# Whole turns of a phase by one write to int32 in place of two float steps, in a gated attention with two gated MLPs

## The chip, the core and the metric

The kernel runs on one core of a Trainium2 chip. Five engines work side by side, each in the order of its own queue: TensorE (PE, with its weight loads as PEld), VectorE (DVE), ScalarE (ACT), GpSimd (POOL) and SyncE (SP, which here only issues DMA transfers). The metric is the device time of one execution in microseconds, lower is better. Times are medians of several runs.

## The reference

The input is q, k, v and complex gates a for 4 x 8 heads, 768 positions and 48 channels. Then come two gated MLPs over 3072 tokens (384 to 2048 to 384).

```python
mag = sqrt(a_re**2 + a_im**2)
scale = minimum(mag, 0.999) / (mag + 1e-6)
a = (a_re + 1j * a_im) * scale                 # per head, position and channel
for t in range(768):
    S = a[:, :, t, :, None] * S + k[t] (outer) v[t]
    y[t] = q[t] @ S.real
x = y as 3072 x 384
x = (h * clip(h + 3, 0, 6) / 6) @ w_out,   h = x @ w_in          # first MLP
x = (h * sigmoid(1.702 * h)) @ w_out,      h = x @ w_in          # second MLP
```

The recurrence is computed in chunks of 128 positions: within a chunk the products of the gates are a decay (the running sum of log magnitudes) and a phase (the running sum of angles). q and k are multiplied by exp(+-decay) and by the cosine and the sine of the phase, and after that the chunk is plain matrix products with a causal mask.

## The kernel before, in words

Twelve batches of 256 positions are prepared (`prep_ops`), each of two chunks; the first batch is prepared in two halves of one chunk each (tokens that end in `.0.0` and `.0.1`), so its tiles are 128 x 384 in place of 128 x 768. The steps of one batch, in the kernel's names: `im2`, `re2` (squares of the gates, ACT), `mag2`, `ln`, `mag`, `inv`, `half`, `eps`, `lneps`, `decay`, `lnhalf`, `invhalf`, `tan`, `scan` (running decay), `E0`, `E1` (its exponentials), `atan`, `carry` (adds the phase left by the batch before), `angle` (running phase), then `round`, `turns`, `frac` (takes whole turns away, so that the sine sees at most half a turn), `keep` (the phase for the next batch), `sin`, `abs`, `cos` on ACT, `qkcos` and `qksin` (q and k times cosine and sine, into the tiles pE and qk).

In `round` (L463) the half angle is scaled to turns and 12582912 is added, which leaves the whole number in the low bits; `turns` (L464) subtracts it again; `frac` (L465) subtracts the whole turns from the scaled angle.

`repE` and `repS` (`repack`, L476 to L486) then copy pE and qk by DMA, SBUF to SBUF, into the tile QK of a chunk, q and k of one head at a time: pE into partitions 0 to 47, qk into 48 to 95. Six transfers make each half. Those of the first batch are spread over three queues: SP, POOL and ACT (tokens `reqE`, `reqS` are ACT's part). With QK there, a chunk runs `kt` (turn k, PE), `sc` (scores, PE), `p` (mask, DVE), `ks` (ACT), `ud`, `pv` (PE), `um`, `ua` (state, DVE), `ysb`, `xp` or `xf`, `xh`, `xl` (its output as high and low part).

An MLP slot is `in` (18 or 9 matmuls, L634), `g1` to `g4` (gate, ACT and DVE) and `out` (L672). Weights come as float32 (`W`, L360, 768 KB each), are taken apart by `da`, `db`, `dc` on DVE (L123, L125, L127), rounded by `hi` on ACT (L380) and left over by `lo` on DVE (L389). `warm_up` (`wm`, L745) is 16 matmuls without use that start when the first cosine is there.

What sets the order: the string PLAN holds one token per step, and DVE, ACT and PE issue in exactly its order, up to the 82nd slot. SP and POOL have no order written out. There a scheduler places the transfers when the program is built, from where it expects the other engines to be. SP issues one transfer after another and stops at the first that has to wait. Transfers issued by SP and by ACT carry one of eight completion semaphores, DMAHW0 to DMAHW7, taken in turn; a transfer that gets one again waits until the transfer that had it before has landed. The tile `a` (gates of a batch, 768 KB, L399) has one buffer, so a batch's load waits for the last reader of the one before.

Of the kernel before, what the change touches and what calls it, by code (L numbers as in the profile page):

```python
# [257 lines left out]
def chunked_path(ctx: ExitStack, tc, flag, a_t, qk_t, v_t, w1i, w1o, w2i, w2o, out):  # L258

    nc = tc.nc  # L260
    V, A, G, T = nc.vector, nc.scalar, nc.gpsimd, nc.tensor
# [591 lines left out]
```

## Time and profile before

| what | before |
|---|---|
| median of 3 runs | 997.92 us (996.52 to 1000.21) |
| profiled execution, its own time | 998.55 us |
| its span, first to last instruction | 996.8 us |
| PE busy | 948.4 us (95%), 5378 matmuls |
| DVE busy | 643.9 us (65%), 919 instructions |
| ACT busy | 517.7 us (52%) |
| POOL busy | 105.8 us (11%) |
| chain that ended last | PE 89%, DVE 5%, ACT 2%, DMA 2% of the span |

How to read it: PE is the long engine, so what matters is where PE is not busy, or busy at a lower granted clock. The page's slices show that at the start alone: the first slice has PE at 1 tenth, the next two at 7 and 5, then 9 to the end; the granted clock is 9, 6, 8 and 9 tenths in the first four slices and 9 after that. DVE is the other way round: 9 tenths and more in slices 3 to 7, 2 to 5 tenths in the last ten. A group's line is line of the kernel, engine, operation, what it writes and reads, and its mean duration.

### The profile page before, as it was taken

The numbers are of one execution on the slowest core, as the hardware profiler recorded it, in microseconds if no ns is written. First come the engines' busy times: TensorE is split into PE (matmuls) and PEld (weight loads), VectorE is DVE, ScalarE is ACT, GpSimd is POOL, SyncE is SP. The second block draws the span as 40 slices with busy tenths as digits, with TensorE's granted clock in tenths as the row PEclk, the third lists the DMA queues.
The fourth block names the chain that finished last, engine by engine and source line by source line (L and its number), as shares of the span: only waits on it lengthen the run. The fifth ranks groups of instructions, "written<-read, shape, count | busy, mean of one in ns | idle before, by whom it ended". The sixth has DMA issues, their size and how long they took to land.

```text
span 996.8 us, 14418 instructions
## 1 busy us (share of the span) xinstructions
PE 948.4 (95%) x5378; PEld 804.8 (81%) x5378; DVE 643.9 (65%) x919; ACT 517.7 (52%) x860; POOL 105.8 (11%) x218
## 2 busy tenths in 40 slices
PE   1759999999999999999999999999999999999996
PEld 1648988998888888888888888888888888888885
DVE  6599999887777766877369984344454544533332
ACT  6376578777677575775325564243343432422332
POOL 1111202213312123031200000000000000000000
PEclk9689999999999999999999999999999999999999
DMA  7956214444443245232337441033353443300001
GB/s 270 283 163 196 66 49 125 131 128 128 122 118 96 72 120 128 80 97 73 72 132 240 159 151 40 1 125 128 127 190 127 158 159 127 111 1 1 32 1 35
DMA packets 70684, 113.63 MB, mean 114 GB/s; under 512 B 9936, under 2 KB 55632, under 8 KB 70608
## 3 DMA queue, kind: packets, MB, share of 16 engines
q1 hardware_dynamic: 63056, 101.02, 32.4%
q0 software_dynamic: 7168, 11.36, 4.3%
q8 instruction: 44, 0.72, 0.3%
q10 hardware_dynamic: 384, 0.26, 0.1%
q14 instruction: 32, 0.26, 0.1%
HBM read 80.22 MB, written 9.44 MB: 90 GB/s over the span
## 4 chain that ended last, share of the span: by engine, by line
PE 89%; DVE 5%; ACT 2%; DMA 2%; issue 1%; SPq 0%; POOL 0%; ACTq 0%; DVEq 0%
PE h L634 38%; PE o L672 38%; PE sc L517 4%; PE ud L563 3%; PE yps L537 3%; PE yps L539 2%; PE kt L526 1%; DMA wr<-in_w1i 1%; DMA QK<-qk 1%; DVE qk L474 1%; DVE pE L473 1%; DMA xf<-ysb 0%; DVE wi L389 0%; DVE pA L436 0%; DVE wx L127 0%
## 5 line engine op out<-in xcount | busy, mean ns | idle before, releaser
L634 PE MATMUL h<-xh,wi 128*128 128x512 f32 (+1 forms) x1248 | 364.9, 376 | 10.8 <-ACT wi L380 6.4
L672 PE MATMUL o<-gh,wo 128*128 128x512 f32 (+1 forms) x1248 | 364.2, 376 | 0.1
L634 PEld LDWEIGHTS h<-xh,wi 128*128 128x128 f32 x1248 | 228.0, 190 | 52.9 <-ACT wi L380 6.6
L672 PEld LDWEIGHTS o<-gh,wo 128*128 128x128 f32 x1248 | 227.2, 189 | 41.7 <-issue 0.9
L634 PE MATMUL h<-xl,wi 128*128 128x512 f32 (+1 forms) x624 | 233.9, 375 | 0.5 <-DVE xl L606 0.4
L672 PE MATMUL o<-gl,wo 128*128 128x512 f32 (+1 forms) x624 | 233.1, 374 | 0.0
L659 DVE TENSOR_TENSOR gl<-tt,gh 128x512 fp32r<-128x512 f32 x192 | 132.2, 690 | 84.0 <-ACT gh L654 83.7
L654 ACT ACTIVATE gh<-tt 128x512 fp32r<-128x512 f32 x192 | 121.0, 632 | 109.3 <-DVE tt L649 65.2
L649 DVE TENSOR_TENSOR tt<-tt,h 128x512 f32<-128x512 f32 x96 | 66.0, 688 | 144.8 <-ACT tt L641 144.8
L641 ACT ACTIVATE tt<-h 128x512 f32<-128x512 f32 x96 | 57.4, 598 | 172.2 <-PE h L634 167.2
L634 PEld LDWEIGHTS h<-xl,wi 128*128 128x128 f32 x624 | 118.3, 190 | 22.2 <-DVE xl L606 1.2
L672 PEld LDWEIGHTS o<-gl,wo 128*128 128x128 f32 x624 | 117.8, 189 | 21.0
L639 ACT ACTIVATE tt<-h,b 128x512 f32<-128x512 f32 x96 | 65.7, 685 | 75.5 <-PE h L634 72.1
L647 DVE SCALAR_TENSOR_TENSOR tt<-tt,h 128x512 f32<-128x512 f32 x96 | 65.2, 683 | 42.4 <-ACT tt L639 42.2
L551 POOL DMA_DIRECT2D xf<-ysb x60 | 30.9, 521 | 242.0 <-ACT ysb L543 232.1
L517 PE MATMUL sc<-QK 96*128 96x128 f32 x384 | 55.0, 291 | 0.0
L517 PEld LDWEIGHTS sc<-QK 96*128 96x128 f32 x384 | 50.8, 203 | 2.2 <-issue 0.7
L486 POOL DMA_DIRECT2D QK<-pE x70 | 35.7, 515 | 157.8 <-DVE pE L473 95.9
L521 DVE TENSOR_TENSOR p<-sc,causal 128x512 f32<-128x512 f32 x48 | 33.0, 688 | 20.7 <-PE sc L517 19.7
L537 PE MATMUL yps<-p,v 128*48 128x128 f32 (+1 forms) x384 | 40.4, 291 | 0.1
L486 POOL DMA_DIRECT2D QK<-qk x70 | 36.4, 526 | 15.6 <-issue 5.8
L603 ACT ACTIVATE xh<-xf 128x384 fp32r<-128x384 f32 x44 | 22.8, 518 | 27.8 <-DMA xf<-ysb 11.5
(111 smaller groups left out, 877.9 us busy)
## 6 DMA issues: line engine op xcount, KB each, us to landing
ws<-in_w2i SPq DMA_DIRECT2D x16, 768.0 KB, 4.4
ws<-in_w2o SPq DMA_DIRECT2D x16, 768.0 KB, 4.5
qk<-in_qk_t SPq DMA_DIRECT2D x48, 192.0 KB, 3.6
a<-in_a_t SPq DMA_DIRECT2D x11, 768.0 KB, 4.6
wr<-in_w1i SPq DMA_DIRECT2D x8, 768.0 KB, 8.3
wr<-in_w1o SPq DMA_DIRECT2D x8, 768.0 KB, 7.8
ws<-in_w1i SPq DMA_DIRECT2D x8, 768.0 KB, 4.4
ws<-in_w1o SPq DMA_DIRECT2D x8, 768.0 KB, 4.6
```

Of the source, the lines that this page charges most:

```text
L486: e.dma_start(out=dst, in_=src)
L517: T.matmul(out=sc[:, i, :], lhsT=kv_(4 * g + i), rhs=qv(4 * g + i), start=True, stop=True)
L521: V.tensor_tensor(out=p, in0=s_["sc", g], in1=causal.unsqueeze(1).to_broadcast([P, 4, CH]), op=ALU.mult)
L537: T.matmul(out=yps[r0:r1, h // 2, :], lhsT=v_c[c][:, e], rhs=s_["p", g][:, i, :], start=True, stop=first)
L634: T.matmul(out=h[:, i, :], lhsT=w[:, k, :], rhs=x[:, k, :], start=(k == 0 and q == 0), stop=(k == 2 and q == 2))
L639: A.activation(out=t, in_=ht[s], func=AF.Relu, bias=b3)
L641: A.activation(out=t, in_=ht[s], func=AF.Sigmoid, scale=1.702)
L647: V.scalar_tensor_tensor(out=t, in0=t, scalar=6.0, in1=ht[s], op0=ALU.min, op1=ALU.mult)
L649: V.tensor_tensor(out=t, in0=t, in1=ht[s], op=ALU.mult)
L654: A.activation(out=hi, in_=gt[s][0], func=AF.Copy)
L659: tail[:] = [V.tensor_tensor(out=lo, in0=gt[s][0], in1=gt[s][1], op=ALU.subtract)]
L672: T.matmul(out=acc[:, o:o + n], lhsT=w[:, e * P:e * P + P], rhs=g[:, i, :], start=(f == o == q == 0), stop=(f == FT - 1 and q == 2), skip_ ...
```

## The change

The two steps `round` and `turns` become one. `round` now only scales, and writes through a view of the same tile as int32, so that the number is rounded as it is written; `frac` reads that tile as int32. The token `turns` goes out of PLAN at all 13 places (11 batches of 768 columns, two halves of 384); nothing else in PLAN is moved. Line numbers after L33 fall by one; `round` keeps L463, and `frac` is L464 now.

```diff
-MAGIC = 12582912.0
...
-turns.0.0 frac.0.0 keep.0.0 abs.0.0 carry.0.1 angle.0.1 sin.0.0 cos.0.0 wm.0 round.0.1 turns.0.1 qkcos.0.0 frac.0.1 repE.0 lo.0 abs.0.1 sin.0.1 keep.0.1
+frac.0.0 keep.0.0 abs.0.0 carry.0.1 angle.0.1 sin.0.0 cos.0.0 wm.0 round.0.1 qkcos.0.0 frac.0.1 repE.0 lo.0 abs.0.1 sin.0.1 keep.0.1
...
-        op("round", lambda: V.tensor_scalar(out=pB(), in0=pA(), scalar1=2.0 / TURN, scalar2=MAGIC, op0=ALU.mult, op1=ALU.add))
-        op("turns", lambda: V.tensor_scalar(out=pB(), in0=pB(), scalar1=MAGIC, scalar2=None, op0=ALU.subtract))
-        op("frac", lambda: V.scalar_tensor_tensor(out=pA(), in0=pA(), scalar=2.0 / TURN, in1=pB(), op0=ALU.mult, op1=ALU.subtract))
+        whole = lambda: pB().bitcast(mybir.dt.int32)
+        op("round", lambda: V.tensor_scalar(out=whole(), in0=pA(), scalar1=2.0 / TURN, scalar2=None, op0=ALU.mult))
+        op("frac", lambda: V.scalar_tensor_tensor(out=pA(), in0=pA(), scalar=2.0 / TURN, in1=whole(), op0=ALU.mult, op1=ALU.subtract))
```

On DVE, in the first batch, this stood before; pA is the running angle, pB the turns, pE and qk what the repack copies:

```order
L463 TENSOR_SCALAR pB<-pA 128x384
L454 TENSOR_SCALAR stat_decay<-pC 128x3
L464 TENSOR_SCALAR pB<-pB 128x384
L465 SCALAR_TENSOR_TENSOR pA<-pA,pB 128x384
L466 TENSOR_SCALAR carry<-pA 128x3
L461 TENSOR_TENSOR pB<-pB,carry 128x3
L436 SCALAR_TENSOR_TENSOR pA<-mask_l,pB 128x384
L463 TENSOR_SCALAR pB<-pA 128x384
L464 TENSOR_SCALAR pB<-pB 128x384
L473 TENSOR_TENSOR pE<-qk,pB 128x6x128
```

And this stands there now, where L464 is `frac`:

```order
L463 TENSOR_SCALAR pB<-pA 128x384
L453 TENSOR_SCALAR stat_decay<-pC 128x3
L464 SCALAR_TENSOR_TENSOR pA<-pA,pB 128x384
L465 TENSOR_SCALAR carry<-pA 128x3
L460 TENSOR_TENSOR pB<-pB,carry 128x3
L435 SCALAR_TENSOR_TENSOR pA<-mask_l,pB 128x384
L463 TENSOR_SCALAR pB<-pA 128x384
L472 TENSOR_TENSOR pE<-qk,pB 128x6x128
```

The two `turns` (the rows of L464 before) are gone, and what is around them stands as it did.

On SP, in the stretch that repacks the first batch, the queue was this before, with what each transfer waits for in brackets (DMAHW0 to 7 are the completion semaphores, DVE and Activation the engines). The first six rows are the copies of pE for chunk 0, the gates `a` of batch 1, the copies of qk for chunk 0 and one of chunk 1:

```order
L486 DMA QK<-pE 48x774 [waits DMAHW6_49,DVE_49]
L486 DMA QK<-pE 16x258 [waits DMAHW7_49]
L399 DMA a<-in_a_t 128x1536 [waits DMAHW1_49,Activation_49]
L486 DMA QK<-qk 48x774 [waits DMAHW7_49,DVE_49]
L486 DMA QK<-qk 16x258 [waits DMAHW2_49]
L486 DMA QK<-qk 48x774 [waits DMAHW3_49,DVE_49]
L486 DMA QK<-qk 16x258 [waits DMAHW4_49]
```

Now the scheduler has placed the same transfers so:

```order
L485 DMA QK<-pE 48x774 [waits DMAHW6_49,DVE_49]
L485 DMA QK<-pE 16x258 [waits DMAHW0_49]
L485 DMA QK<-qk 48x774 [waits DMAHW2_49,DVE_49,Activation_49]
L485 DMA QK<-qk 16x258 [waits DMAHW5_49]
L398 DMA a<-in_a_t 128x1536 [waits DMAHW7_49,Activation_49]
L485 DMA QK<-qk 48x774 [waits DMAHW3_49,DVE_49]
L485 DMA QK<-qk 16x258 [waits DMAHW4_49]
```

The load of `a` has moved behind the two copies of qk for chunk 0, and the semaphores are dealt out anew. On ACT, whose order is unchanged, the first five of its own copies now wait for these:

```order
L485 DMA QK<-pE 32x258 [waits DMAHW7_49]
L485 DMA QK<-pE 32x258 [waits DMAHW1_49]
L485 DMA QK<-qk 32x258 [waits DMAHW4_49,DMAHW5_49,DMAHW3_49,DVE_49]
L485 DMA QK<-qk 32x258 [waits DMAHW4_49]
L485 DMA QK<-pE 32x258 [waits DMAHW6_49,DVE_49]
```

So the first of them holds DMAHW7, which the load of `a` waits for. Further on, SP differs at one place: the next `a` load (batch 2) stands one weight load earlier. POOL, ACT and PE have the same rows as before.

## Rows read from the trace of the kernel before

**Rows 1.** Busy time by stretch: us, busy (instructions) per engine, granted clock, DMA, GB/s.

```profile
core 0: us, PE busy (x) PEld busy (x) DVE busy (x) ACT busy (x) POOL busy (x), PEclk, DMA share, GB/s
22.00:36.00 14.00, 7.04 (x37) 6.88 (x38) 9.92 (x15) 1.44 (x3) 4.49 (x8) 0.80 0.65 160
36.00:58.00 22.00, 21.33 (x142) 18.31 (x141) 13.57 (x19) 14.16 (x25) 0.00 (x0) 0.66 0.73 267
58.00:72.00 14.00, 5.02 (x36) 4.41 (x35) 13.65 (x18) 11.41 (x17) 1.47 (x3) 0.85 0.53 182
72.00:100.00 28.00, 27.06 (x238) 24.73 (x239) 26.56 (x39) 18.58 (x33) 4.93 (x10) 0.89 0.69 192
464.00:980.00 516.00, 516.00 (x2384) 427.17 (x2383) 273.06 (x399) 195.49 (x324) 10.55 (x21) 1.00 0.31 101
```

**Rows 2.** DVE in the timeline of the first batch: start us, us, instruction.

```profile
19.36 0.36 DVE L464 TENSOR_SCALAR pB<-pB 128x384 f32<-128x384 f32 x1
22.21 0.36 DVE L464 TENSOR_SCALAR pB<-pB 128x384 f32<-128x384 f32 x1
24.77 0.95 DVE L474 TENSOR_TENSOR qk<-qk,pC 128x768 f32<-128x768 f32 x1
```

**Rows 3.** DMA issues in the same timeline (ACTq, SPq, POOL), in order of time.

```profile
24.51 0.63 ACTq L486 DMA_DIRECT2D QK<-pE  x1
24.82 0.54 SPq L399 DMA_DIRECT2D a<-in_a_t  x1
26.28 1.02 POOL L486 DMA_DIRECT2D QK<-qk  x2 [1.40 <-ACT pB L331]
28.12 6.49 SPq L486 DMA_DIRECT2D QK<-qk  x4
```

**Rows 4.** What SP's queue waited for from 23 to 30 us: total, times, longest.

```profile
SPq L486 <- DMA QK<-pE: 2.7, 1, 2.7
```

**Rows 5.** Transfers issued 23 to 25 us: KB, us from issue to landing.

```profile
a<-in_a_t SPq DMA_DIRECT2D x1, 768.0 KB, 8.3
QK<-pE SPq DMA_DIRECT2D x1, 145.1 KB, 3.4
QK<-pE POOLq DMA_DIRECT2D x1, 145.1 KB, 3.9
QK<-pE ACTq DMA_DIRECT2D x1, 32.2 KB, 6.0
```

**Rows 6.** The same, issued 28.1 to 30 us.

```profile
QK<-qk SPq DMA_DIRECT2D x1, 145.1 KB, 6.8
```

**Rows 7.** The timeline where PE starts, and the first users of batch 1's gates.

```profile
22.00 6.14 PE L745 MATMUL warm<-pB,ident 128*128 128x128 f32 x32 [22.00 <-ACT pB L331]
35.09 0.88 PE L526 MATMUL kt<-ident,QK 96*128 96x96 f32 x4 [6.96 <-DMA QK<-qk]
39.53 0.83 ACT L336 ACTIVATE pB<-a 128x768 f32<-128x768 f32 x1
43.65 0.95 DVE L442 TENSOR_TENSOR pA<-pA,pB 128x768 f32<-128x768 f32 x1
44.44 2.08 PE L517 MATMUL sc<-QK 96*128 96x128 f32 x8
```

**Rows 8.** The timeline of batch 1's phase, and the matmul that waits for it.

```profile
64.01 0.56 DVE L464 TENSOR_SCALAR pB<-pB 128x768 f32<-128x768 f32 x1
72.68 0.58 PE L634 MATMUL h<-xh,wi 128*128 128x256 f32 x1 [2.88 <-DVE wi L389]
```

**Rows 9.** Granted clock around PE's start (columns as in rows 1).

```profile
30.00:32.00 2.00, 0.00 (x0) 0.00 (x0) 1.99 (x3) 0.00 (x0) 0.00 (x0) 0.57 1.05 216
50.00:52.00 2.00, 2.00 (x25) 1.53 (x23) 2.00 (x3) 0.64 (x2) 0.00 (x0) 0.81 1.02 421
```

**Rows 10.** DVE groups by shape: count, busy us, mean ns, idle before.

```profile
L436 DVE TENSOR_TENSOR_SCAN pA<-mask_p,pB 128x768 f32<-128x768 uint8 x11 | 19.3, 1755 | 1.1 <-ACT pB L331 1.0
L465 DVE SCALAR_TENSOR_TENSOR pA<-pA,pB 128x768 f32<-128x768 f32 x11 | 10.5, 953 | 0.1
L123 DVE TENSOR_SCALAR wx<-wr 128x768 uint32<-128x768 uint32 x16 | 8.6, 553 | 0.4 <-DMA wr<-in_w1i 0.4
L464 DVE TENSOR_SCALAR pB<-pB 128x768 f32<-128x768 f32 x11 | 6.1, 556 | 0.2
```

More of the change, by code (lines that the diff above doesn't have):

```diff
@@ L46 @@
 mag.1 kt1.1 db.1 pv1.1 ks1.1 half.1 eps.1 xp.0 dc.1 ysb.1 lneps.1 ud.1 da.2 lnhalf.1 decay.1 xp.1 xh.0 scan.1 invhalf.1 xh.1 tan.1 E0.1 xl.0 E1.1 xl.1 lastE.1
-ua.1 lastqk.1 in.0 tab2.1 qkE.1 atan.1 um.1 in.2 hi.1 La.2 carry.1 low.1 Lv.2 angle.1 g1.0 W.11 W.10 W.12 g1.2 W.13 round.1 W.8 turns.1 frac.1 lo.1 abs.1 db.2
+ua.1 lastqk.1 in.0 tab2.1 qkE.1 atan.1 um.1 in.2 hi.1 La.2 carry.1 low.1 Lv.2 angle.1 g1.0 W.11 W.10 W.12 g1.2 W.13 round.1 W.8 frac.1 lo.1 abs.1 db.2
 sin.1 cos.1 keep.1 dc.2 qkcos.1 hi.2 re2.2 tab1.2 qksin.1 repE.2 im2.2 lo.2 W.14 repS.2 g2.0 in.1 mag2.2 g3.0 g4.0 ln.2 g2.2 W.15 out.0 inv.2 Lv.4 da.8 Lv.3
@@ L50 @@
 invhalf.2 pv1.2 g4.2 ud.2 scan.2 ysb.2 Lq.2 xp.2 ua.2 E0.2 low.2 um.2 sc0.3 xh.2 db.5 E1.2 kt0.3 sc1.3 p0.3 ks0.3 xl.2 kt1.3 lastE.2 p1.3 lastqk.2 pv0.3 ks1.3
-dc.5 tab2.2 pv1.3 da.6 tan.2 ud.3 ysb.3 hi.5 db.6 xp.3 atan.2 lo.5 carry.2 out.1 dc.6 xh.3 xl.3 hi.6 da.7 angle.2 in.4 lo.6 round.2 g1.4 in.3 db.7 turns.2 dc.7
+dc.5 tab2.2 pv1.3 da.6 tan.2 ud.3 ysb.3 hi.5 db.6 xp.3 atan.2 lo.5 carry.2 out.1 dc.6 xh.3 xl.3 hi.6 da.7 angle.2 in.4 lo.6 round.2 g1.4 in.3 db.7 dc.7
 out.2 g1.3 ua.3 hi.7 g2.3 frac.2 g3.3 in.7 g4.3 abs.2 g2.4 sin.2 lo.7 cos.2 qkE.2 out.3 g3.4 g1.7 g4.4 tab1.3 in.6 qkcos.2 keep.2 repE.4 qksin.2 out.4 g1.6
@@ L57 @@
 lnhalf.3 g4.12 invhalf.3 pv1.5 lo.13 scan.3 out.11 ysb.5 xf.5 tan.3 E0.3 in.13 low.3 E1.3 xl.4 da.15 lastE.3 lastqk.3 qkE.3 tab2.3 out.12 atan.3 db.15 g1.13
-in.15 La.4 angle.3 xh.5 g2.13 in.14 round.3 g3.13 turns.3 g1.15 g4.13 g1.14 frac.3 out.13 xl.5 abs.3 g2.14 sin.3 g2.15 in.16 cos.3 dc.15 keep.3 g3.14 qkcos.3
+in.15 La.4 angle.3 xh.5 g2.13 in.14 round.3 g3.13 g1.15 g4.13 g1.14 frac.3 out.13 xl.5 abs.3 g2.14 sin.3 g2.15 in.16 cos.3 dc.15 keep.3 g3.14 qkcos.3
 g3.15 in.17 hi.15 qksin.3 repE.6 im2.4 tab1.4 in.18 g4.14 repS.6 g1.16 g4.15 lo.15 g1.17 g1.18 clip.4 out.14 repS.7 g2.16 re2.4 g2.17 g3.16 mag2.4 out.15
@@ L61 @@
 xf.6 sc0.7 lnhalf.4 um.6 sc1.7 invhalf.4 p0.7 Lv.7 g3.18 kt0.7 Lv.8 p1.7 in.19 ks0.7 scan.4 xh.6 kt1.7 tan.4 lastE.4 pv0.7 lastqk.4 ks1.7 xl.6 E0.4 pv1.7 g4.18
-E1.4 low.4 ud.7 ysb.7 qkE.4 y1.15 xf.7 y2.15 tab2.4 out.16 ua.7 um.7 atan.4 carry.4 La.5 angle.4 out.17 xh.7 g1.19 xl.7 round.4 in.21 turns.4 frac.4 g2.19
+E1.4 low.4 ud.7 ysb.7 qkE.4 y1.15 xf.7 y2.15 tab2.4 out.16 ua.7 um.7 atan.4 carry.4 La.5 angle.4 out.17 xh.7 g1.19 xl.7 round.4 in.21 frac.4 g2.19
 abs.4 out.18 keep.4 clip.5 g3.19 cos.4 g4.19 in.20 sin.4 qkcos.4 g1.21 re2.5 qksin.4 out.19 g1.20 im2.5 g2.20 repS.9 in.23 g2.21 g3.20 g3.21 g4.20 tab1.5 g4.21
@@ L65 @@
 sc1.8 ks0.8 g2.22 Lq.5 kt1.8 p1.8 g3.22 pv0.8 ks1.8 g4.22 pv1.8 scan.5 ud.8 ysb.8 xf.8 tan.5 E0.5 in.24 ua.8 E1.5 low.5 um.8 lastE.5 Lv.9 lastqk.5 qkE.5 tab2.5
-sc0.9 out.22 atan.5 p0.9 g1.24 carry.5 angle.5 xh.8 kt0.9 sc1.9 ks0.9 round.5 kt1.9 p1.9 out.23 ks1.9 turns.5 frac.5 g2.24 abs.5 pv0.9 xl.8 g3.24 keep.5 pv1.9
+sc0.9 out.22 atan.5 p0.9 g1.24 carry.5 angle.5 xh.8 kt0.9 sc1.9 ks0.9 round.5 kt1.9 p1.9 out.23 ks1.9 frac.5 g2.24 abs.5 pv0.9 xl.8 g3.24 keep.5 pv1.9
 cos.5 g4.24 in.25 sin.5 qkcos.5 ysb.9 xf.9 ud.9 qksin.5 g1.25 tab1.6 in.27 repE.10 ua.9 um.9 g2.25 out.24 g3.25 repS.10 g1.27 g4.25 xh.9 g2.27 in.26 xl.9 g3.27
@@ L70 @@
 scan.6 invhalf.6 out.26 g1.29 g4.28 E0.6 tan.6 E1.6 pv0.11 g2.29 lastE.6 lastqk.6 qkE.6 out.27 tab2.6 atan.6 low.6 pv1.11 g3.29 angle.6 in.30 ysb.11 xh.10
-xf.11 g4.29 round.6 out.28 xl.10 g1.30 turns.6 g2.30 frac.6 g3.30 in.31 g4.30 abs.6 keep.6 xh.11 out.29 cos.6 xl.11 sin.6 qkcos.6 g1.31 in.32 tab1.7 g2.31
+xf.11 g4.29 round.6 out.28 xl.10 g1.30 g2.30 frac.6 g3.30 in.31 g4.30 abs.6 keep.6 xh.11 out.29 cos.6 xl.11 sin.6 qkcos.6 g1.31 in.32 tab1.7 g2.31
 repE.13 qksin.6 g3.31 out.30 g1.32 La.7 g4.31 repS.12 g2.32 in.33 g3.32 g4.32 repS.13 out.31 g1.33 g2.33 Lv.12 g3.33 in.34 repE.12 y0.31 g4.33 y1.31 clip.7
@@ L75 @@
 in.36 ks1.13 invhalf.7 low.7 E0.7 tan.7 out.34 g1.36 E1.7 g2.36 g3.36 pv0.13 lastE.7 g4.36 lastqk.7 tab2.7 pv1.13 qkE.7 ud.13 atan.7 ysb.13 carry.7 angle.7
-in.37 xh.12 xf.13 round.7 out.35 La.8 g1.37 turns.7 g2.37 frac.7 g3.37 in.38 g4.37 abs.7 ua.13 sin.7 keep.7 um.13 out.36 xl.12 g1.38 cos.7 g2.38 g3.38 qkcos.7
+in.37 xh.12 xf.13 round.7 out.35 La.8 g1.37 g2.37 frac.7 g3.37 in.38 g4.37 abs.7 ua.13 sin.7 keep.7 um.13 out.36 xl.12 g1.38 cos.7 g2.38 g3.38 qkcos.7
 in.39 xh.13 tab1.8 g4.38 out.37 qksin.7 g1.39 im2.8 g2.39 repS.14 in.40 xl.13 g3.39 g4.39 clip.8 out.38 repE.14 g1.40 re2.8 g2.40 g3.40 mag2.8 in.41 repE.15
@@ L79 @@
 half.8 in.43 lnhalf.8 scan.8 invhalf.8 out.41 g1.43 tan.8 E0.8 g2.43 kt1.14 lastE.8 low.8 g3.43 sc1.14 ks1.14 g4.43 E1.8 in.44 p1.14 lastqk.8 qkE.8 tab2.8
-ud.14 g1.44 atan.8 g2.44 sc0.15 g3.44 carry.8 out.42 g4.44 angle.8 pv0.14 round.8 pv1.14 p0.15 turns.8 in.45 ysb.14 ua.14 xf.14 um.14 frac.8 kt0.15 g1.45
+ud.14 g1.44 atan.8 g2.44 sc0.15 g3.44 carry.8 out.42 g4.44 angle.8 pv0.14 round.8 pv1.14 p0.15 in.45 ysb.14 ua.14 xf.14 um.14 frac.8 kt0.15 g1.45
 sc1.15 keep.8 ks0.15 g2.45 out.43 p1.15 g3.45 abs.8 g4.45 xh.14 kt1.15 in.46 ks1.15 xl.14 cos.8 sin.8 qkcos.8 pv0.15 g1.46 pv1.15 tab1.9 g2.46 ud.15 qksin.8
@@ L85 @@
 p0.17 g3.51 ud.16 low.9 ysb.16 g4.51 E1.9 xf.16 tan.9 sc1.17 lastE.9 lastqk.9 ua.16 tab2.9 out.49 um.16 Lv.17 p1.17 atan.9 in.52 angle.9 xh.16 round.9 pv0.17
-g1.52 xl.16 pv1.17 g2.52 turns.9 g3.52 out.50 ysb.17 g4.52 xf.17 frac.9 qkE.9 in.53 abs.9 sin.9 cos.9 keep.9 out.51 g1.53 tab1.10 g2.53 qkcos.9 in.54 g3.53
+g1.52 xl.16 pv1.17 g2.52 g3.52 out.50 ysb.17 g4.52 xf.17 frac.9 qkE.9 in.53 abs.9 sin.9 cos.9 keep.9 out.51 g1.53 tab1.10 g2.53 qkcos.9 in.54 g3.53
 xh.17 g4.53 repE.19 out.52 qksin.9 g1.54 g2.54 repS.19 in.55 xl.17 g3.54 g4.54 out.53 La.10 g1.55 repE.18 g2.55 g3.55 in.56 g4.55 repS.18 out.54 g1.56 im2.10
@@ L90 @@
 in.60 lastE.10 g4.59 lastqk.10 tab2.10 qkE.10 pv0.18 atan.10 pv1.18 ud.18 g1.60 carry.10 angle.10 ysb.18 xf.18 out.58 g2.60 um.18 g3.60 Lv.19 round.10 sc0.19
-Lv.20 g4.60 La.11 kt0.19 turns.10 in.61 ks0.19 p0.19 frac.10 xh.18 xl.18 out.59 keep.10 g1.61 abs.10 g2.61 g3.61 in.62 cos.10 g4.61 sin.10 qkcos.10 sc1.19
+Lv.20 g4.60 La.11 kt0.19 in.61 ks0.19 p0.19 frac.10 xh.18 xl.18 out.59 keep.10 g1.61 abs.10 g2.61 g3.61 in.62 cos.10 g4.61 sin.10 qkcos.10 sc1.19
 g1.62 kt1.19 p1.19 out.60 ks1.19 g2.62 qksin.10 g3.62 im2.11 pv0.19 tab1.11 g4.62 pv1.19 clip.11 in.63 ysb.19 re2.11 xf.19 mag2.11 out.61 g1.63 repE.20 ln.11
@@ L95 @@
 y2.63 E0.11 ud.20 g1.66 E1.11 g2.66 sc0.21 g3.66 out.64 lastE.11 g4.66 lastqk.11 tab2.11 qkE.11 pv0.20 atan.11 pv1.20 carry.11 sc1.21 ua.20 ysb.20 p0.21 xf.20
-kt0.21 in.67 um.20 ks0.21 p1.21 angle.11 kt1.21 g1.67 out.65 ks1.21 g2.67 round.11 g3.67 turns.11 xh.20 in.68 g4.67 frac.11 xl.20 abs.11 pv0.21 keep.11 g1.68
+kt0.21 in.67 um.20 ks0.21 p1.21 angle.11 kt1.21 g1.67 out.65 ks1.21 g2.67 round.11 g3.67 xh.20 in.68 g4.67 frac.11 xl.20 abs.11 pv0.21 keep.11 g1.68
 pv1.21 cos.11 g2.68 ud.21 sin.11 qkcos.11 g3.68 out.66 ysb.21 g4.68 xf.21 qksin.11 in.69 ua.21 um.21 out.67 g1.69 repE.23 g2.69 g3.69 in.70 xh.21 g4.69 repE.22
```

## The prediction, on record before the run

> **What bounds the kernel now.** I read the busy times by stretch first. From 464 to 980 us PE is busy 516.00 of 516 us at full clock: whatever DVE saves there or in the long middle, PE hides. PE has holes only at the start [rows 1]: it is busy 7.04 of 14 us from 22 to 36, and 5.02 of 14 from 58 to 72, while DVE is busy 13.65 of 14 in that second stretch. From 36 to 58 PE is busy 21.33 of 22, but at a mean clock of 0.66. So the end moves by what the start moves, and I looked for what ends each hole.
>
> The first ends at 35.09: the first matmuls on real data (kt, chunk 0) had waited 6.96 us, at last for a copy QK<-qk [rows 7]. The second ends at 72.68, released by DVE [rows 8].
>
> **The first hole is a queue, not VectorE.** qksin of chunk 0 ends at 24.77 + 0.95 = 25.72 [rows 2], but SP issued its copy of qk only at 28.12, because SP had waited 2.7 us for the landing of an earlier copy QK<-pE [rows 3, 4]; the semaphore it needed was held. And when issued it took 6.8 us to land, 28.12 + 6.8 = 34.9, against 3.4 for a copy of the same 145 KB issued before the 768 KB load of `a` went out at 24.82 [rows 3, 5, 6]. The load of `a` is thus in front of what PE waits for. In the changed program it stands behind the two copies of qk for chunk 0, and the first of these waits for a semaphore whose last holder is a weight load from the very start. That is the larger part of what this change does, though no line of the diff says so.
>
> **Part by part.**
>
> *Two steps of 128x384 removed in the first batch*: 0.36 + 0.36 = 0.72 us of a dense DVE run before qksin [rows 2]; ACT's sine and cosine follow frac and come as much earlier. qksin of chunk 0 then ends at 25.0.
>
> *The copies of chunk 0*: SP issues at 25.0 in place of 28.12. At the undisturbed 3.4 us it lands at 28.4. POOL's copy, issued at 26.28 [rows 3], goes at 25.56 and lands, at the 3.9 us of POOL's copy of pE [rows 5], at 29.5. ACT's pieces are small (32 KB); the one issued just before `a` took 6.0 us, which I put down to `a`, and take 3.9 for it. So QK of chunk 0 is complete at 29.5 and kt starts at 29.6: 5.5 us earlier. Bounds: with 3.4 for the last copy 29.0, a gain of 6.1; with the 6.8 us kept even without `a`, 25.56 + 6.8 = 32.4, a gain of 2.7.
>
> *The load of `a`* now waits for ACT's first copy: issued at 24.51 - 0.72 = 23.8, landed at 27.7 (29.8 by 6.0). At its 8.3 us `a` lands at 36.0 (38.1). Its first user, the square at 39.53, would come at 34.0 if ACT moves with PE, so ACT waits some 2.0 us. Two squares of 0.83 end at 41.2 in the run before, and what reads them starts at 43.65 [rows 7]: 2.4 us of slack, which covers the 2.0. By the bound of 38.1 it is 1.7 short. Cost taken: 0.
>
> *Chunk 1's copies* on SP stand behind `a`. The scores of chunk 1 start at 44.44 [rows 7], then 38.9. If SP's copies move only once `a` has landed, 36.0 + 3.4 = 39.4, 0.5 late; if they share with it, not late. Taken: 0.
>
> *One step of 128x768 removed in batch 1*: 0.56 us, in the run of DVE that ends in the left-over of a weight for which PE waits at 72.68 [rows 8]. DVE is 13.65 of 14 us busy there, so it counts in full: 0.56.
>
> *Ten more of them* (of 11, 6.1 us in all [rows 10]): 5.6 us of DVE behind a PE that is busy 27.06 of 28 us from 72 to 100 and wholly later [rows 1]. Worth 0; at best the 0.94 us of holes from 72 to 100.
>
> *The int32 write and read* appear in no row. The write is bounded by the 556 ns of the step removed and, if it goes at the pace of a two-source step, 953 [rows 10]. I take 556, since a step of this kind that writes 4-byte integers (L123) takes 553. Below that nothing of this kind and size exists. frac reads int32 beside f32: 953 as now, or up to the 1755 of the scan, which reads uint8 beside f32. I take 953. The upper ends cost 0.2 + 0.2 + 0.4 and 0.4 + 0.4 + 0.8 us at the three places that count, 2.4 in all.
>
> **Sum.** 5.5 + 0.56 = 6.1 us. The profiled execution takes 998.55, so 992.4; against the median of 997.92 I forecast **991.8**. Its own range: down to 990.3, with 6.1 for the copies and the 0.94 us of holes won as well (7.6), and up to 994.0, with `a` 1.7 and chunk 1 0.5 late (3.9).
>
> **Rivals.**
>
> *The clock stays up.* In the run before, PE idles 6.96 us after the warm-up ends at 28.14, the granted clock falls to its half (1.2 GHz) within 30 to 32, and comes back only within 50 to 52 (0.81 over that stretch is half speed until 50.8) [rows 7, 9]. The warm-up would now end at about 27.4 and kt start at 29.6, a gap of 2.2 us. If the clock lasts over it, the 15.7 us from 35.1 to 50.8 run up to twice as fast: at most 7.8 us more. `a` at 36.0 and chunk 1's copies at 39.4 hold PE back, so I put half of it, 3.8: 991.8 - 3.8 = 988.0. Against it: the clock was already down within 30 to 32, soon after the warm-up, and 15 us of attention matmuls did not bring it back. The Trainium skill (TensorE: Matmul & The Clock Gate, "Why this matters for your kernels") advises to leave no long idle gaps between bursts of matmuls, since the clock is taken back after one; by that rule the shorter gap is worth more than its length, and the trace agrees in that the clock fell in this hole.
>
> *The copies are slow for a reason of their own* (small pieces, three queues on the same DMA engines, which were 0.65 busy from 22 to 36 [rows 1]), and 6.8 us stays their time: 2.7 + 0.56 = 3.3, 994.6. Against: 3.4 and 3.9 us for the copies that went first.
>
> *The change doesn't do what it says*: int32 takes the slow pace at both steps. 6.1 - 2.4 = 3.7: 994.2. Against: L123.
>
> *Slower: `a` comes late.* It now waits for a landing, and goes out beside chunk 1's copies on all three queues, with ACT standing at its first square and everything of chunk 1 behind it on ACT. Loss begins at 34.0 + 2.4 = 36.4 and the gain is used up when `a` lands at 42.5, 14.8 us after its issue. At twice its 8.3 us it lands at 44.3: 1.8 us slower than before, 999.7. For it: the bound above already passes 36.4. Against: 8.3 us was measured with all three queues at work.
>
> **How the numbers follow.** Forecast 0.40; clock stays 0.30; copies slow 0.16; int32 slow 0.08; `a` late 0.06. A measurement of this kernel can tell about 0.5% (5.0 us) from no change: the line is at 992.9 and 1002.9. The forecast's own range lies two thirds below 992.9 (0.27); with the clock's 0.29 and 0.02 of the others, faster is 0.58. Slower by that much needs `a` 11 us later than I think, or a stretch at half clock that gets longer: 0.03. The rest, 0.39, is within. The range goes from 987.0, a little below the clock's case, to 997.0, which leaves out half of its lower tail and the late `a`.
>
> **What would show it.** After: kt of chunk 0 starting near 29.6, released by a copy of POOL or ACT; SP's copy of qk issued near 25.0 and landing in under 4.5 us; `a` issued near 27.7; round at 0.36 and 0.56 and frac at 0.95 as before; the first matmul after the second hole near 66.6; PE without holes after that, with the same busy time from there to the end. If kt starts before 31 and the time is still above 995, the gain was given back between 30 and 66, and `a` is the first suspect. If kt starts at 34 or later, I am wrong about the queue.

## The result, and the profile after

The median went from 996.55 us (996.15 to 1000.55, seven runs) to 989.31 (986.12 to 994.23, seven runs), a ratio of 0.9917 with an interval of 0.9894 to 0.9939. The spread of the new kernel has grown to 8 us, and the profiled execution is its slowest: 994.23 us, span 992.5. Its spread has a section of its own below.

The stretches, as in [rows 1]:

```profile
22.00:36.00 14.00, 11.37 (x88) 10.55 (x87) 12.42 (x19) 4.55 (x8) 4.48 (x8) 1.00 0.68 170
36.00:58.00 22.00, 19.04 (x124) 15.33 (x124) 16.11 (x21) 16.40 (x29) 0.00 (x0) 0.77 0.69 243
58.00:72.00 14.00, 6.50 (x32) 6.20 (x33) 13.24 (x16) 10.50 (x15) 5.51 (x11) 0.63 0.98 305
72.00:100.00 28.00, 25.74 (x248) 23.23 (x247) 24.86 (x37) 16.93 (x30) 0.52 (x1) 1.00 0.50 144
464.00:980.00 516.00, 515.91 (x2359) 426.97 (x2359) 270.86 (x394) 192.62 (x320) 10.51 (x21) 1.00 0.31 101
```

PE has 4.3 us more of work in the first. From 58 to 72 it still stands for 7.5 us. Between 36 and 58 it is idle for 3.0 us, half of it (from 56.5 on) the start of the second hole, which has moved forward. Between 72 and 100 it is idle for 2.3 us, nearly all of it in one hole that is new.

The timeline of DVE and of the transfers at the start, the answer to [rows 2, 3]:

```profile
18.95 0.36 DVE L463 TENSOR_SCALAR pB<-pA 128x384 int32<-128x384 f32 x1
19.34 0.56 DVE L464 SCALAR_TENSOR_TENSOR pA<-pA,pB 128x384 f32<-128x384 f32 x1
23.96 0.95 DVE L473 TENSOR_TENSOR qk<-qk,pC 128x768 f32<-128x768 f32 x1
24.97 1.15 SPq L485 DMA_DIRECT2D QK<-qk  x2
27.87 0.34 SPq L398 DMA_DIRECT2D a<-in_a_t  x1
```

The write to int32 takes the 0.36 us that the step to float32 took, and qk goes out from SP at 24.97, before `a`, where it went at 28.12, after it. SP's copies of 145 KB landed so (KB, us from issue to landing; the first issued 24 to 25 us, the others 28 to 31):

```profile
QK<-qk SPq DMA_DIRECT2D x1, 145.1 KB, 3.3
...
QK<-qk SPq DMA_DIRECT2D x1, 145.1 KB, 7.5
QK<-pE SPq DMA_DIRECT2D x1, 145.1 KB, 6.5
```

Chunk 0's takes 3.3 us in place of 6.8 [rows 6]; those of chunk 1, now issued right behind `a`, take 7.5 and 6.5. PE, ACT and DVE in the timeline, the answer to [rows 7, 8]:

```profile
28.34 0.30 PE L525 MATMUL kt<-ident,QK 96*128 96x96 f32 x1 [0.51 <-DMA QK<-qk]
29.24 0.44 PE L525 MATMUL kt<-ident,QK 96*128 96x96 f32 x3 [0.59 <-DMA QK<-qk]
33.55 1.09 PE L536 MATMUL yps<-p,v 128*64 128x128 f32 x16
35.88 0.84 ACT L335 ACTIVATE pB<-a 128x768 f32<-128x768 f32 x1 [3.14 <-DMA a<-in_a_t]
36.73 1.84 PE L516 MATMUL sc<-QK 96*128 96x128 f32 x8 [2.09 <-DMA QK<-pE]
37.68 0.96 DVE L441 TENSOR_TENSOR pA<-pA,pB 128x768 f32<-128x768 f32 x1 [2.92 <-ACT pA L335]
51.60 0.51 PE L633 MATMUL h<-xh,wi 128*128 128x256 f32 x2 [0.67 <-ACT xh L602]
66.08 0.58 PE L633 MATMUL h<-xh,wi 128*128 128x256 f32 x1 [2.88 <-DVE wi L388]
74.94 1.13 PE L516 MATMUL sc<-QK 96*128 96x128 f32 x8 [2.23 <-issue]
```

The first real matmul comes at 28.34 in place of 35.09, the second hole ends at 66.08 in place of 72.68: 6.60 us earlier. Then PE stands 2.23 us before the scores of batch 1, where it did not stand before. 6.60 - 2.23 = 4.37, and the two profiled executions differ by 998.55 - 994.23 = 4.32: in this execution everything is accounted for.

### The profile page after: what moved, and what is told of

It is laid out like the page before. It is cut to its first block, busy times and chain, and to the rows that moved or that the text cites. A ratio compares the mean times of both kernels' runs of the same rounds, so it can differ in the third digit from the quotient of the medians.

```text
span 992.5 us, 14408 instructions
## 1 busy us (share of the span) xinstructions
PE 946.4 (95%) x5378; PEld 801.4 (81%) x5378; DVE 638.0 (64%) x906; ACT 517.1 (52%) x860; POOL 104.8 (11%) x218
## 4 chain that ended last, share of the span: by engine, by line
PE 86%; DVE 5%; DMA 4%; ACT 2%; issue 1%; SPq 0%; POOL 0%; ACTq 0%; DVEq 0%
PE o L671 37%; PE h L633 37%; PE sc L516 4%; PE ud L562 2%; PE yps L536 2%; PE yps L538 2%; DMA wr<-in_w1i 1%; PE kt L525 1%; DMA a<-in_a_t 1%; DMA wr<-in_w1o 1%; DMA xf<-x2d 1%; DMA xf<-ysb 0%; DVE pE L472 0%; DMA QK<-pE 0%; DVE tt L646 0%
## 5 line engine op out<-in xcount | busy, mean ns | idle before, releaser
L516 PE MATMUL sc<-QK 96*128 96x128 f32 x384 | 53.0, 284 | 4.3 <-issue 2.2
```

The source lines that it names most:

```text
L516: T.matmul(out=sc[:, i, :], lhsT=kv_(4 * g + i), rhs=qv(4 * g + i), start=True, stop=True)
```

## The same program with and without a fall of the clock

The same program was run again beside later experiments: ten times, 992.28 us in the median, 985.62 to 996.56; ratio 0.9935 (0.9913 to 0.9958). Its second profile is of an execution of 986.83 us. The granted clock from 36 to 38 and from 46 to 48 us in the first profile, and then from 36 to 38 in the second (columns as in [rows 1]):

```profile
36.00:38.00 2.00, 1.27 (x7) 1.30 (x8) 0.32 (x1) 2.00 (x5) 0.00 (x0) 0.74 0.58 143
46.00:48.00 2.00, 2.00 (x9) 0.68 (x8) 0.94 (x1) 1.76 (x3) 0.00 (x0) 0.70 1.05 422
```

```profile
36.00:38.00 2.00, 2.00 (x19) 2.00 (x20) 1.29 (x2) 2.00 (x5) 0.00 (x0) 1.00 0.91 313
```

And PE's timeline in the second:

```profile
27.92 0.30 PE L525 MATMUL kt<-ident,QK 96*128 96x96 f32 x1 [0.94 <-DMA QK<-qk]
35.93 1.13 PE L516 MATMUL sc<-QK 96*128 96x128 f32 x8 [1.70 <-DMA QK<-pE]
46.27 0.50 PE L633 MATMUL h<-xh,wi 128*128 128x256 f32 x2 [0.67 <-ACT xh L602]
60.75 0.58 PE L633 MATMUL h<-xh,wi 128*128 128x256 f32 x1 [2.87 <-DVE wi L388]
67.47 1.05 PE L516 MATMUL sc<-QK 96*128 96x128 f32 x8
```

In the first, PE waits 2.09 us for copies, until 36.73; the clock falls to 1.2 GHz within 36 to 38 and is back only within 46 to 48. In the second the wait is 1.70 and the clock stays at 2.4 GHz until the second hole. The first MLP matmul comes 51.60 - 46.27 = 5.33 us earlier there, and the hole of 2.23 is missing: 7.56 us, against 7.40 between the two times. Of the 5.33 us, 0.42 are there at kt already (28.34 and 27.92) and 4.53 arise in chunk 1, where PE takes 14.87 us from the scores to the first MLP matmul at the lower clock and 10.34 at the higher. Of the 17 executions of this program five take 985.6 to 988.4 at a mean clock of 0.993, ten 991.6 to 996.6 at 0.986 to 0.992, two lie between; the median of all is 991.9.

## The experiments

Each ran five rounds against the kernel before; the ratio is to the runs of before on the same chip at the same time. In the edits `after(x, y)` orders x behind y, and `mark` keeps the transfers issued: E and S for SP's copies of pE and qk by chunk, a and w for loads.

**E1, three steps, new queue.** The kernel before; batch 1's load of `a` made to go behind SP's copies of qk, later weights held behind chunk 1's:

```diff
+            if b == 1:
+                after(mark["a", b], mark["S", 0])
```

> The kernel before with its three VectorE steps kept; only SP's queue is in the order that the changed kernel has: batch 1's load of a behind SP's two copies of qk of chunk 0. Theory Q (the queue made the gain): the copy of qk lands some 3.4 us after its issue at 25.7, kt of chunk 0 starts near 29.1 instead of 35.09, 0.7 us behind the changed kernel (two steps of 0.36 more), and the second hole ends 0.56 + 0.7 us behind it: 989.3 + 1.3 = 990.6 us, range 988 to 993. Theory S (the steps made the gain, the queue is a side effect that is worth nothing): kt still starts near 35, and the time stays at 996.5, range 995 to 998.

993.38 us (990.59 to 999.49), ratio 0.9953 (0.9933 to 0.9974): neither number. SP's and PE's timeline say why: a load of v had slipped in.

```profile
24.91 0.60 SPq L416 DMA_DIRECT2D v<-in_v_t  x1
25.92 2.88 SPq L490 DMA_DIRECT2D QK<-qk  x2
30.58 0.55 PE L532 MATMUL kt<-ident,QK 96*128 96x96 f32 x4 [1.88 <-DMA QK<-qk]
```

SP's copy took 4.6 us, kt came at 30.58 and not 29.1, and the clock fell within 30 to 32. So I repeated it without that load.

**E9, three steps, v held.** As E1, and

```diff
+        if c == 2:
+            after(r, mark["E", 1])
```

> The kernel before with three VectorE steps and the changed kernel's order on SP, as in the run e1, but with the 192 KB load of v, which in e1 had slipped in front of SP's copies of qk, held behind the copies of chunk 1, where the changed kernel has it. Theory Q (the order on SP makes nearly all of the gain, the steps their own 1.3 us): kt of chunk 0 starts near 29.1, released 0.7 us after the changed kernel's 28.34, and the time is that of the changed kernel in the same call plus 1.3 us. Theory D (the 0.72 us of the two steps decide more than their length, since the kt that comes later finds the clock falling): kt near 29.1 but the clock falls within 30 to 34 us, as in e1, and the time stays near e1's 993.4, 3 us or more above the changed kernel. If kt starts at 30.5 again, the load of v was not what made e1 late.

988.95 us (987.66 to 992.59), ratio 0.9921 (0.9899 to 0.9944), beside the changed kernel's 0.9935 on the same chip. PE in the timeline:

```profile
28.58 0.30 PE L534 MATMUL kt<-ident,QK 96*128 96x96 f32 x1 [1.52 <-DMA QK<-qk]
36.06 1.13 PE L525 MATMUL sc<-QK 96*128 96x128 f32 x8 [1.19 <-DMA QK<-pE]
46.27 0.50 PE L642 MATMUL h<-xh,wi 128*128 128x256 f32 x2 [0.67 <-ACT xh L611]
61.34 0.58 PE L642 MATMUL h<-xh,wi 128*128 128x256 f32 x1 [2.88 <-DVE wi L391]
```

With all three VectorE steps kept, the order on SP gives all of the gain that the times can show. Theory D falls: the clock stays up, and the time is not above the changed kernel's. My 1.3 us is neither seen nor excluded, since each of the two intervals is 0.45% wide. Against the second profile of the changed kernel, in which the clock stays up too, the steps show at their places: kt 0.66 us later, lost again by the wait for chunk 1 (the first MLP matmul is at 46.27 in both), the second hole 0.59 later, for which the times of these two executions leave room (987.66 and 986.83).

**E2, two steps, old queue.** The changed kernel, `a` back in front of the copies of qk, which are tied behind it (that tie, and later weights held as in E1, are not shown here):

```diff
-cos.0.1 qksin.0.0 reqE.0 qkcos.0.1 repS.0 reqS.0 qksin.0.1 W.5 da.3 La.1 reqE.1
+cos.0.1 qksin.0.0 reqE.0 qkcos.0.1 La.1 repS.0 reqS.0 qksin.0.1 W.5 da.3 reqE.1
...
+            if b == 1:
+                after(mark["a", b], mark["E", 0])
```

> The changed kernel with its two steps; only SP's queue is put back: batch 1's load of a in front of SP's copies of qk of chunk 0, as in the kernel before. Theory Q: the copy of qk is again issued near 28 or takes 6 to 7 us, kt starts at 34 to 35, and what is left of the gain is the steps' own 0.72 + 0.56 = 1.3 us: 996.5 - 1.3 = 995.2 us, range 993.5 to 997. Theory S: all of the gain stays, 989.3 us, range 987 to 991.5.

997.97 us (994.95 to 1000.22), ratio 0.9995 (0.9979 to 1.0012): the steps alone change nothing that can be measured. It is 1.0 us under the 998.96 of before in the same comparison, and the interval holds theory Q's 1.3 us as well as 0. SP and PE in the timeline, with the landing of SP's copy:

```profile
24.18 0.54 SPq L400 DMA_DIRECT2D a<-in_a_t  x1
27.50 6.45 SPq L489 DMA_DIRECT2D QK<-qk  x4
34.28 0.90 PE L533 MATMUL kt<-ident,QK 96*128 96x96 f32 x4 [5.91 <-DMA QK<-qk]
...
QK<-qk SPq DMA_DIRECT2D x1, 145.1 KB, 6.7
```

Issue at 27.50, 6.7 us to land, kt at 34.28, as before to within the 0.8 us of the steps. E9 and E2 together show the cause, the order on SP; E6 below splits it in two.

**E3, weight first.** The changed kernel, with weights 10 to 12 tied ahead of batch 2's `a`:

```diff
+            if b == 2:
+                for i in (10, 11, 12):
+                    after(mark["a", b], mark["w", i])
```

> The changed kernel, with one weight load put back in front of batch 2's load of a, where the kernel before had it. Theory W (the new hole in PE from 72.7 to 74.9 us comes of SP's repack of batch 1 waiting for a weight load that the change moved close in front of it): SP's wait of 3.2 us before that repack shortens by about 2 us, the hole goes, and the time falls by 2.2 us: 987.1 us, range 985 to 989. Rival B (from 62 to 78 us the DMA engines are full, and the order within the same bytes changes nothing): the hole stays or moves to another place of the same length, 989.3 us, range 987.5 to 991.

987.53 us (985.96 to 991.5), ratio 0.9905 (0.9882 to 0.9928). That is theory W's number, but the unchanged program takes it too in some executions. The profile has no hole of 2.2 us (0.31), and neither has the second profile of the unchanged program. Theory W is not shown. What the hole goes with is the landing of one copy of 145 KB of batch 1: 8.9 us in the first profile after, 8.3 in E1 and 7.9 in E2 (holes of 2.2, 2.4 and 2.1), 7.6 in E9 (1.0), 6.2 to 6.8 in the second profile after, E3 and E4 (0 to 0.3), 6.6 and 6.8 in E12 and E14 (0.8). E2 has the weight in front of `a`, and the hole all the same. All three holes of over 2 us are in profiles in which the clock had fallen before, but it had also fallen in those of the kernel before, E6, E12 and E15, where this hole is 0 to 0.8. Why the copy is slow there stays open.

**E4, longer warm-up.** The changed kernel with 20 matmuls in place of 16.

```diff
-        for i in range(16):
+        for i in range(20):
```

> The changed kernel with 20 matmuls of warm-up in place of 16, some 1.6 us more of PE work of which about 0.5 us falls into a gap that PE has anyway, so that kt starts up to 1.1 us later. Theory C1 (the granted clock falls within 36 to 38 us because PE waits there for chunk 1's copies, 2.1 us): the longer warm-up changes nothing there, the clock falls at the same place, and the time is the same or up to 1 us more: 990.0 us, range 988 to 992. Theory C2 (the clock falls because the warm-up's work is some time past): it falls about 1.5 us later or not in this stretch, and the time is 986 to 988 us.

988.48 us (987.08 to 990.77), ratio 0.9909 (0.9889 to 0.9929). In its profile PE waits 1.96 us before chunk 1's scores and the clock stays, where in E1 it fell after a wait of 1.88 and in E7 (below) it stays over one of 2.21: the length of a wait alone does not foretell the fall. Undecided between C1 and C2.

**E10** is the changed kernel again, told above.

> The changed kernel once more, unchanged, beside the other runs of this call, so that they can be compared with it on the same chip: 989.3 us, range 987.5 to 991.5. Its profile falls on another execution: if the spread of the changed kernel (986.1 to 994.2) is the clock's, the granted clock of this execution either falls within 36 to 38 us again, with a time of 992 to 994, or stays at 1.00 to about 54, with the first FFN matmul near 47 in place of 51.6 and a time of 986 to 988.

The median of 992.28 is above my range; both kinds of executions came, and the profiled one is of the second kind.

**E6, `a` first.** The changed kernel with batch 1's `a` ahead of all copies, in the plan (taken out of its old place further down, with W.5) and by a tie; later weights are held as in E1.

```diff
-lastE.0.0 tan.0.0 E0.0.1 tan.0.1 E1.0.1 dc.0 lastE.0.1 lastqk.0.0 lastqk.0.1 tab2.0 qkE.0.0 qkE.0.1 atan.0.0 atan.0.1 angle.0.0
+lastE.0.0 tan.0.0 E0.0.1 tan.0.1 E1.0.1 dc.0 lastE.0.1 lastqk.0.0 lastqk.0.1 tab2.0 qkE.0.0 qkE.0.1 atan.0.0 atan.0.1 W.5 La.1 angle.0.0
...
+                        if b == c == y == 0:
+                            after(r, mark["a", 1])
```

> The changed kernel with batch 1's load of a put in front of chunk 0's first copies, right behind the weight loads, when the DMA engines have nothing to do (0.06 busy from 22 to 24 us), instead of behind the copies of qk. Theory A (the late a, for which ACT waits 3.1 us, and the copies behind it, for which PE waits 2.1 us at 36.7, cost about 2 us and the clock's fall): both waits go, scores of chunk 1 start near 34.6, the clock stays up past 50 in every execution, and the time is 985.5 us, range 983.5 to 987.5. Rival: a now shares the DMA engines with the copies of pE and takes their semaphore, the copies of chunk 0 land 1 to 3 us later, kt starts at 30 or later after a gap in which the clock falls, and the time is 991 us or more.

996.14 us (992.93 to 998.33), ratio 0.9977 (0.996 to 0.9994). The rival was right, by its semaphore: SP waited 2.7 us for its own earlier copy, as before [rows 4], and issued qk at 28.04. It was wrong on the sharing, since `a`, issued at 18.51, had landed by 24.6, and the copy of qk, issued at 28.04, landed so:

```profile
QK<-qk SPq DMA_DIRECT2D x1, 145.1 KB, 3.7
```

That splits the cause. Without `a` beside it the copy takes 3.7 us where E2's takes 6.7, and kt comes at 31.78, 2.5 us before E2's; the rest, 31.78 - 28.34 = 3.44 us, is mostly the issue, 28.04 in place of 24.97. So the held semaphore and the load of `a` each cost about 3 us at kt. Chunk 1's copies, too, take no more than 3.1 us here, and PE does not wait for them, in E6 or in E7.

**E7, three edits.** E6 with E3's order and 20 matmuls of warm-up.

```diff
-        for i in range(16):
+        for i in range(20):
...
+            if b == 2:
+                for i in (10, 11, 12):
+                    after(mark["a", b], mark["w", i])
```

> The changed kernel with three things at once: batch 1's load of a in front of chunk 0's copies (as in e6), one weight load back in front of batch 2's load of a (as in e3) and 20 matmuls of warm-up in place of 16 (as in e4). Theory A with the clock kept up: no waits of PE between 29 and 46 us, first FFN matmul near 45, 984.5 us, range 982.5 to 987. Rival: as in e6, the copies of chunk 0 land later, and the time is 990 us or more.

987.62 us (986.55 to 989.86), ratio 0.9901 (0.988 to 0.9921): neither number, but beside E6 the price of the clock. The first is E6, the second E7: where kt starts, the clock from 30 to 32, the first MLP matmul.

```profile
31.78 0.90 PE L533 MATMUL kt<-ident,QK 96*128 96x96 f32 x4 [3.66 <-DMA QK<-qk]
...
30.00:32.00 2.00, 0.22 (x2) 0.22 (x2) 1.55 (x2) 0.00 (x0) 0.00 (x0) 0.58 0.73 211
...
54.31 0.50 PE L641 MATMUL h<-xh,wi 128*128 128x256 f32 x2 [0.67 <-ACT xh L610]
```

```profile
31.52 0.55 PE L536 MATMUL kt<-ident,QK 96*128 96x96 f32 x4 [2.21 <-DMA QK<-qk]
...
30.00:32.00 2.00, 0.48 (x5) 0.48 (x6) 1.42 (x2) 0.00 (x0) 0.00 (x0) 1.00 0.70 200
...
47.19 0.50 PE L644 MATMUL h<-xh,wi 128*128 128x256 f32 x2 [0.67 <-ACT xh L613]
```

kt starts within 0.3 us of each other; in E6 PE had idled 3.66 us and the clock fell, in E7 2.21 and it stayed, and 16 us later E7 is 7.1 us ahead. The Trainium skill's advice against long idle gaps between bursts of matmuls (TensorE: Matmul & The Clock Gate, "Why this matters for your kernels") agrees with this pair.

**E12, long warm-up before**, and **E15**, the same on E2.

```diff
-        for i in range(16):
+        for i in range(32):
```

> The kernel before, with nothing changed but the warm-up: 32 matmuls in place of 16, which should end near 33.6 us and leave a gap of some 1.5 us before kt of chunk 0 in place of 6.96 (the added matmuls are not used for the output). Theory K (most of what the order on SP gives comes through the granted clock, which no longer falls in the first hole): kt still starts near 35.1, the clock stays at 1.00 to past 55, the first FFN matmul comes near 51 in place of 57.6, and the time falls by 6 to 7 us: 992 us, range 990 to 994, with less spread than before. Rival L (it is the earlier kt itself that counts, the clock is secondary or comes back by itself): 997 us, range 995.5 to 999.

> The two VectorE steps with the old order on SP (as in the run e2), and 32 matmuls of warm-up. Beside the run of the kernel before with the same warm-up it shows what the steps are worth by themselves when the clock does not fall in either. Theory Q: 0.72 us at kt and 0.56 us in batch 1, at most 1.3 us under the other run, 991 us; since chunk 1's copies can take the first part back, 0.6 us is as likely. Theory S (the steps are worth more than their length): 3 us or more under it.

E12: 999.56 us (992.19 to 1001.05), ratio 0.9988 (0.9966 to 1.0011). E15: 996.77 (990.53 to 1000.15), ratio 0.997 (0.9948 to 0.9992). Both fail as tests. I had reckoned 0.36 us for one matmul of the warm-up; 32 took 8.91 us in E12, 0.28 each (10.08 in E15):

```profile
21.76 8.91 PE L745 MATMUL warm<-pB,ident 128*128 128x128 f32 x64 [21.76 <-ACT pB L331]
34.59 0.56 PE L526 MATMUL kt<-ident,QK 96*128 96x96 f32 x4 [3.93 <-DMA QK<-qk]
...
34.00:36.00 2.00, 1.41 (x10) 1.44 (x11) 0.00 (x0) 0.79 (x2) 0.00 (x0) 0.80 0.60 145
```

The gap stayed at 3.93 us in E12's profile and at 2.69 in E15's, and the clock fell within 34 to 36 in both. The three best executions of E12, with mean clocks of 0.988 to 0.992, take 992.2 to 993.3, what theory K said; the median does not, and is above rival L's range too. E15's median is 2.8 us under E12's, close to theory S's 3, but its mean only 1.3, and the two overlap over nearly their whole spread, so they don't tell what the steps are worth.

**E13, filler**, and **E14**, filler with 20 matmuls of warm-up. In both one weight load stands ahead of batch 2's `a`, as in E3: in E14 by E3's tie, in E13 without one, since the scheduler put it there. The diff is E13's; E14 has 20 for 16.

```diff
-    def warm_up():
+    def warm_up(more):
...
-        for i in range(16):
+        for i in range(5 if more else 16):
...
-kt1.0 sc1.0 p0.0 ks1.0 hi.3 ud.0 p1.0 lo.3 im2.1 pv0.0 um.0 pv1.0 re2.1
+kt1.0 sc1.0 p0.0 ks1.0 hi.3 ud.0 p1.0 lo.3 im2.1 pv0.0 um.0 pv1.0 wm.1 re2.1
```

> The changed kernel with 5 matmuls of the warm-up's kind put between chunk 0's last matmuls and the scores of chunk 1, where PE waits 1.7 to 2.1 us for copies (they are not used for the output); one weight load goes ahead of batch 2's load of a, as in the run e3, with which this is to be compared. Theory K (the spread of the changed kernel is the clock falling, or not, in that wait): the clock stays up in every execution, none lies above 989, and the median is 986.8 us, range 985.5 to 988.5. Rival: the executions spread from 986 to 992 as in e3, 987.5 or more in the median; the clock falls for another reason.

> The changed kernel with the three edits that the runs so far speak for: 20 matmuls of warm-up, 5 more before the scores of chunk 1, one weight load ahead of batch 2's load of a. Theory K: no fall of the clock before 54 us in any execution, 986.5 us, range 985.5 to 988. Rival: no better than e3 and e4 alone, 987.5 to 988.5.

E13: 988.26 us (987.45 to 988.82), ratio 0.9889 (0.9869 to 0.9909). E14: 988.58 (988.23 to 992.78), ratio 0.99 (0.9877 to 0.9923). PE and ACT in E13's timeline and the clock:

```profile
34.49 1.38 PE L744 MATMUL warm<-pB,ident 128*128 128x128 f32 x10
35.95 0.84 ACT L335 ACTIVATE pB<-a 128x768 f32<-128x768 f32 x1 [3.29 <-PE warm L744]
36.41 1.13 PE L516 MATMUL sc<-QK 96*128 96x128 f32 x8 [0.54 <-DMA QK<-pE]
47.31 0.50 PE L633 MATMUL h<-xh,wi 128*128 128x256 f32 x2 [0.67 <-ACT xh L602]
...
36.00:38.00 2.00, 1.59 (x15) 1.62 (x16) 0.25 (x1) 2.00 (x5) 0.00 (x0) 1.00 0.91 356
```

With PE at work in the wait, all six executions of E13 stay within 1.4 us, at mean clocks of 0.992 to 0.994. The spread is gone, as theory K said; the median is 1.5 us above its number. Half of that is the filler's own: it reads pB, which batch 1's first square on ACT overwrites, so that square started at 35.95, behind the filler, though `a` had landed at 34.5. DVE was late with chunk 1's mask behind it, PE waited 0.66 us for that, and the first MLP matmul comes 0.74 us after E3's 46.57. One of E14's six lies at 992.78, so the filler is no guarantee. E13 is the best ratio of all, 1.1% under the kernel before; its interval ends at 0.9909, those of the changed kernel begin at 0.9894 and 0.9913, so it beats that one by 0.3 to 0.5% if at all.

## Why the prediction was right, point by point

- **The first hole is a queue.** Right, and shown: E9 has all of the gain that can be measured without the change in arithmetic, E2 none of it with the change. Both halves of the account, the held semaphore and the load of `a`, show by themselves in E6.
- **Two steps of 0.36 us off DVE.** Right at its place: qksin ends at 24.91 (25.0 expected). In the time it shows nowhere: chunk 1's copies take it back.
- **The copies of chunk 0, kt 5.5 us earlier.** Issue 24.97, landing 3.3: as expected. kt began at 28.34, since the heads came in parts, and went on at 29.24 (29.6 expected): 5.9 to 6.8 earlier.
- **`a`, cost 0.** Issue 27.87 and landing near 35.8 (36.0 expected). ACT waited 3.14 us for it and DVE 2.92 behind ACT, more than the 2.0 and the 2.4 that I had set against each other, yet PE waited for neither in this profile. The cost stands to within 0.2 us, which PE lost behind the same wait in E4, at full clock.
- **Chunk 1's copies, cost 0.** Mis-sized, but not late for the reason I gave. Forecast were a landing by 39.4 and scores at 38.9. The copies went out at 28.61 and 30.11 and shared with `a`; they took 7.5 and 6.5 us, not 3.4, and still landed at 36.1 and 36.6, and the scores began at 36.73, 2.2 us earlier than forecast. But PE was ready at 34.64, because the clock had not fallen, and waited 2.09 us, where 0.5 was my upper end. The cost of 0 holds for a PE at half clock alone. That the load of `a` slows the copies beside it, as it did those of chunk 0 before, shows in E6 and E7: there `a` has landed first, and PE does not wait.
- **One step of 0.56 us in batch 1.** Right at its place, in every profile. Before, the first MLP matmul stood so:

```profile
57.60 0.51 PE L634 MATMUL h<-xh,wi 128*128 128x256 f32 x2 [0.67 <-ACT xh L603]
```

From there to the end of the second hole it was 72.68 - 57.60 = 15.08 us, and 15.07 in E1, E9 and E12, which keep the step; with the step gone it is 14.48 or 14.49 in all ten profiles. In the time of whole runs these 0.6 us can't be told.
- **Ten more steps, 0.** Nothing of the runs speaks against it: PE is busy 515.91 of 516 us from 464 to 980.
- **int32.** The write takes 561 ns and frac 952, by the groups of the page. Rival "int32 slow" falls.

```profile
L463 DVE TENSOR_SCALAR pB<-pA 128x768 int32<-128x768 f32 x11 | 6.2, 561 | 0.2
L464 DVE SCALAR_TENSOR_TENSOR pA<-pA,pB 128x768 f32<-128x768 f32 x11 | 10.5, 952 | 0.1
```

- **The clock.** This is the step of the forecast that failed; at the first hole its rival was right. The forecast had the clock fall in the first hole, as before. It did not: from kt to the end of chunk 0's matmuls PE took 34.64 - 28.34 = 6.3 us, where 9.35 had passed from kt to chunk 1's scores before [rows 7]. These 3 us pay for the 2.09 of chunk 1 and more, so that the scores come 44.44 - 36.73 = 7.71 us earlier. Then the two kinds of executions part. Where the clock falls in the wait for chunk 1, PE takes 14.87 us to the first MLP matmul, against 13.16 before, and 6.00 us are left there; where it stays up, 57.60 - 46.27 = 11.33. So the sum of 6.1 us came near in the first kind by luck, since two terms that were left out or set at 0, the clock in chunk 0 and the wait in chunk 1 with its fall, go against each other. The second kind, 985.6 to 988.4, is my rival of 988.0. The median of 989.31 mixes the two and lies below the forecast's own range (990.3 to 994.0); that of the repetition, 992.28, lies within it.
- **PE without holes after 66.6.** Wrong: 2.23 us before batch 1's scores. I had not priced that hole; the second move on SP, by which I would explain it, is not shown to be its cause (E2, E10).
- **Rival "`a` comes late".** It landed at 35.8, before the 36.4 where a loss was to begin. **Rival "copies slow for a reason of their own"**: fell, by 3.3 us at chunk 0 and by E6.

## What to carry to other kernels

When a scheduler deals out queues and semaphores, taking an instruction away can move transfers that have nothing to do with it: compare the queues before and after, not only the lines. Undo the reordering by itself and keep the arithmetic, and the other way round; only that pair showed here that what can be measured of the gain is the order's. What the arithmetic is worth, 0.6 us, shows at one place of the profiles and not in the times. And look at what an added instruction reads: E13's filler, on an idle engine, held up ACT by reading a tile that ACT was to overwrite. And read slack on an engine beside the granted clock of its neighbour, since it shrinks when that clock stays up.
